# A new table of order and engines for the 3118 operations of one attention and gated-MLP kernel

## The chip, the core and the metric

The kernel runs on one core of a Trainium2 chip, in one launch. The metric is device time in microseconds; three runs of the kernel before gave 518.59, 518.84 and 520.0, with a median of 518.84. A core has five engines that work side by side, each through its own queue in order: TensorE (PE in the profile), VectorE (DVE), ScalarE (ACT), GpSimd (POOL) and SyncE (SP), which here only issues DMAs. An engine waits at an instruction until the semaphores that it names have arrived; whatever stands behind it in the same queue waits too.

## The reference, cut to what matters

Inputs are q, k, v of shape (8 batches, 8 heads, 576 positions, 64), and the weights of a gated feed-forward layer.

```python
scores = scale * np.matmul(q, k.transpose(0, 1, 3, 2))
mask_local = (rel >= 0) & (rel < stride)                                 # heads 0 to 3, stride 32
mask_strided = (rel >= 0) & (pos[None, :] % stride == pos[:, None] % stride)   # heads 4 to 7
attn = softmax(where(mask, scores, -1e9));  x = concat_heads(attn @ v)   # (8, 576, 512)
h = np.maximum(x @ w_in, 0.0);  u, v = h[..., :512], h[..., 512:]
v_n = (v - mean(v)) / np.sqrt(var(v) + 1e-06)
v_s = np.einsum('ts,bsd->btd', w_spatial, v_n) + b_spatial[None, :, None]
return (u * v_s) @ w_out                                                 # (8, 576, 512)
```

## The kernel before, in words

**What is computed where.** The heads are taken in pairs, four pairs t to a batch: pairs 0 and 1 are local, 2 and 3 strided, 32 pairs in all. For a pair TensorE makes the scores of small blocks (line 543 for local pairs, 689 for strided ones) into a PSUM bank. VectorE brings them out (580 or 705; the first four pairs with reductions at 563 and 714), ScalarE takes the exponentials (600, 726), VectorE or GpSimd divides by the sums (505), VectorE turns blocks of 32 x 32 (624, 743), and small copies, twelve for a local pair and four for a strided one (called moves here, line 405 on ScalarE and 407 on the other two), put the turned blocks into `ptl` or `pts`. TensorE then multiplies with v (653, 759), and the result is brought out as `x`.

**Two parts of a number.** The big matmuls work on rounded numbers, so each operand is kept as a rounded part and the rest. `rnd` (lines 405 and 407) writes the rounded part, with one input, on ScalarE, VectorE or GpSimd. `rest` (line 415) subtracts it from the number, with two inputs, on VectorE or GpSimd. `combine` (line 880) makes sums and differences of blocks, also with two inputs. `evac` (427 on ScalarE, 429 on VectorE) copies a PSUM bank out.

**The feed-forward part.** For each batch `v_tile` (1012) multiplies x with w_in, `chain` normalises it: relu on ScalarE (970), mean and variance on VectorE (975 to 983), a power on GpSimd (988), and the scaling on VectorE (995). `moe_1` makes u at 1212 for batches 0 to 2, `moe_u` at 1135 for batches 3 to 7. `moe_2` multiplies with w_spatial (1309, 1321, 1322), gates u with the result (1332 and 1334, VectorE), and multiplies with w_out (1413); VectorE adds the products (1441), and SyncE stores them (1434).

**What sets the order.** Every operation is recorded by `add` with the engines that may do it. Nothing plans at build time: a text `ORDER` holds one word for each of the 3118 operations. A word is the step to the next operation's number and, where there is a choice, a letter for the engine (A ScalarE, V VectorE, G GpSimd), and `*n` for n filler matmuls ahead of it. `order` reads the words and `emit` issues the operations in just that order, so the table fixes each engine's queue; it keeps every dependency in front of what needs it:

```python
n += int(step) + 1
e = dict(zip("PAVGS", ENGINES))[engine] if engine else given[0]
issued.append((n, e))
```

The buffers do not depend on the table: `Ring` hands out a fixed number of them in the order in which operations are recorded. PSUM has four banks `m`, two `s` and two `po`; SBUF has four buffers `o` and two `vv` from which results are stored. An operation that writes a ring's buffer waits for all users of what stood there before, stores included. The `port` argument of `add` names operations of VectorE and GpSimd that share a way into SBUF; nothing in this file reads it.

Of the kernel before, what the change touches and what calls it, by code (L numbers as in the profile page):

```python
# [220 lines left out]
-246G -48A 28 -106 -35 110A 302 -301A -6A -31 35A -10G 33 -34A -3V 140 144 -276A 24V -34A 270 -57 -212A 0A
127V 161 -164 -74 -51 197 -174 181A -205 121 -100G -26A 55 -54A 23G -2A -26 295 -294 23A 98 79G -151 -8A -22
28 66A -67V 66G 71V 63 -203 -31A 30 -30A 45 -162A 144 -32 19G 11 144 -203 267 -242 -161 213 -205A 201 -5 193
-197 -25 -48 71 765 -759 174 -346V 167 189 21 -235V 134 -191A 289 -235 134A -191G 201 73 -10 -14 -188 209 -79
-127 194 -78G -326 214 173 -197A 238 -430 215 -29A 241 -31 -104 -84 172 46 -246A 211 -192 177 -58V -38 140
-249A 30 170 12 -395 422 -227 230 -224 176 12A 28 -428V 245 139A 12V -71 -144 200V -178 119V 73 -78 104 -221
32 188 -104 -134 648 -413 -20 -162 -255 434 -32 -74G -119 222 -10 -138 -39 -48 210 21 -106G 628 -526 1 -451A
268 633 -679 228 -39 -72G -79 3 80V -347A 448 -28 -81V 102 -182 -12 192 -178 167 -218 123V 105 -193 -38G 189
-145 179 -197 199 -197 92A 74 -87V 115 -2 5 -197 -268V 467 -212 -256A 426 34 -238 231 -108G 2A 104 -200 -256V
462 -125A 71 -147 201 -276A 157V -344A 404 42 3 -36 -172 206 -239A 125V 115 -123V -74 81V 116 -279A -194V 415A  # L230
55 -130V 115 -43V 46 -109 116 -242A -222 284 131A 54 -249A -42 294 -61G 44 -120V 112 -207 227 -295 34A 259 -23
5 -129G -78 213 -255A 245 15 -220 -41G 243 -250A 45 85 134 -488V 469 -243A 264 -144V -2 -364 239V 267 -24
-251A 266 -138 -134A 258 17 -277V 253A -207V 23 180A -244 244V 462 -585 -122 121V 489 -485A -6 133 448 -461
411 -623 87G 133 -12 -200G 204 -120A 113 15 -136G 2A 121 4 -222A 226 -206 -16G -48A 268 -142V 3A 142 -149V
-125A 129G 483 -356 -219A 92V 2A -99G 95A 131 -223A 575 -562 217 -143G 490 -360 -143V 142 -138G 490 -334A -12
335 3 -355 -223A 226 20G 325 -479A 133 -136V -103A 243 -280 138G 140 340 -331V -255A 243 1 8G -11 12A -12 -15
22A -21 -277 47A 251G -257A 232 21V -258A 235 9 338 -331G -19 40 -20V 19 -10G -24 -227V 226 11A 20 307 -10
-319G 19 -22V -254 584 -345 -239 264V -268A 568 -308V 28 -38V 16A 22 287 -309A -7V -14G 19 -17A 16 -264 243V
-2V 22 -3A -18V 19 2A -26V 19 16 287 -320V 552 -537A 10 -8V -21A 31 -35V 18 296 -287 317 -346G 343 -322A -276
566 72 -369G -272 559 -277 320 56 -93 38 -325 -5 280 -294G 13 268 -267 319 -316 311 -329G 335 -320 311 -333V  # L240
339 -324 325 -15 -329G 297 -276 -4 308 -615A 308 274 40 -613 302 -319 15G 302 -19 309 -308 7 274G 24 -299 -298
606 32 -350 -290A -17 311 -296G -3A 886 -293 7 -300 291 -295 -8 316 -305 -306V 606 29 -350 13 -8 246 -542 565
-287 293V 0A 2G 79 -89A 0V 267 -264G -574V 565A 3G 219 -478 255A 86 -92G -568A 303 261G 32 -599 634 -310 248V
60G -635 301 302 -308 276 30 0V -30 -3A 79 -22 -300 271 21 -336 7 275V 38G 280 -284V 3G -296 254 -277 595
-244G -39V -10A -298 564 -243 -25G -4V 48 -311 265A -38 -264 296G 1V 3A -313 9 299G 43 132 -156 -322 343 -344
303 211 -31 -180 -319 527 -528 501 -15 -488 502 -486 478 -181A 12 168 -186A -314 27 468 -489 320V 156 -448
-40A 490 -141 -22 -314 484 -151V -310 -43V 38 3 271 -299 468 -443 437 -152A -314 26 287A -307 304V -3A 157
-481 19 283 -267 -38 342 -306 -38 29 7 -38V 29 292 -323V 16 495 -172G 128 -454 325A -308 447 30 37 -232V -284
476 -188 187 -474 476 5 -522 11 18 487 -519 11 509 -490 -33 315V -287 10 424 -455 20 300A -301 437 -427 471 -5
-478 430 -427 -8 2 439 -432 422 -428 437 23 -24 -444 -39 481G -433 -12 276 -270 -47A 520 -468 275A -276 426  # L250
-441 -42V 489A -5G -441 -5 6 457 -20V -439 470 -10 -503 472A -429 426V 2A -420 425V 20 -27V -432 255 190 -20A
8V -483V 534 -500 -36V 44 275 183 529 -540 -451 430A 558 -998 7 431V 71 -228A -265 -117 95 14 451 -556 113 430
-54 -373 437 -463 12 -13 6 -7 11 -6 -7A 21 -22A 0V 13 0 -6 -6 15 -16 15 -12 4 -5 10 458 -458 432 -442 31V 433
-458 -9 8 456G -461 3 21V -20 427G 25 -454 239 -4A -241 25A -19 15A -16 12A 2V -16 12G -23 9 229 -230 15G -15
# [24 lines left out]
-8 -3 12 477 -473 0 -7 -5 4 5 441V 11 -470 469 -455 441V -449 6 -13 282A -264 -8 430A 31 -2 -470 459 -453 462
# [1405 lines left out]
```

## Time and profile before

| | |
|---|---|
| median of 3 runs | 518.84 us (518.59 to 520.0) |
| profiled execution, its own time | 519.92 us |
| its span in the profile | 518.0 us |
| busy: PE, PEld, DVE, ACT, POOL | 495.0, 449.6, 414.8, 263.1, 227.1 us |
| bytes moved by DMA | 52.65 MB |
| TensorE's granted clock over the span | 0.984 of full speed |

All durations below come from that one execution. PE is the matmuls, PEld the loading of their weights beside them. A matmul's end is modelled and matmuls are pipelined, so PE counts as busy while one follows another; its idle time is what the waits list. "Idle before, releaser" says for how long an engine stood idle ahead of an instruction and what it was waiting for.

### The profile page before, as it was taken

How to read it: one execution, taken by the hardware profiler on the slowest of the kernel's cores; microseconds unless marked ns; L12 is line 12 of the kernel's file. 1: busy time of each engine (PE TensorE's matmuls, PEld its weight loads, DVE VectorE, ACT ScalarE, POOL GpSimd, SP SyncE). 2: the span in 40 equal slices, each digit the busy share in tenths (PEclk: the TensorE clock that was granted, in tenths of full speed). 3: DMA queues.
4: the chain of work that ended last, by engine and by line, in shares of the span. 5: the costliest groups of instructions: out<-in, count | busy, mean ns of one | idle time of the engine just before them, and what ended most of it. 6: DMA issues, size and time to landing. Idle time of an engine off the chain costs nothing.

```text
span 518.0 us, 14629 instructions
## 1 busy us (share of the span) xinstructions
PE 495.0 (96%) x5816; PEld 449.6 (87%) x5816; DVE 414.8 (80%) x1154; ACT 263.1 (51%) x778; POOL 227.1 (44%) x265
## 2 busy tenths in 40 slices
PE   6599999999999999988989999999999999999997
PEld 4378998889998898988889987989899998999897
DVE  5689999996676889985899779897698957895456
ACT  3699977556561686462534545354464413231221
POOL 2344566422174348462355734656146404421342
PEclk9679999999999999999999999999999999999999
DMA  8948432541304504162052503125020210011002
GB/s 274 407 177 321 153 114 77 181 137 66 101 15 126 185 2 134 27 195 71 9 171 72 185 4 122 58 84 175 1 97 1 79 56 2 0 35 59 0 1 92
DMA packets 26244, 52.65 MB, mean 102 GB/s; under 512 B 3136, under 2 KB 11584, under 8 KB 26176
## 3 DMA queue, kind: packets, MB, share of 16 engines
q1 hardware_dynamic: 26176, 51.72, 30.0%
q8 instruction: 46, 0.75, 0.6%
q14 instruction: 22, 0.18, 0.1%
HBM read 42.27 MB, written 9.44 MB: 100 GB/s over the span
## 4 chain that ended last, share of the span: by engine, by line
PE 67%; DVE 17%; issue 4%; DMA 4%; POOL 3%; ACT 3%; SPq 2%; DVEq 0%; POOLq 0%; ACTq 0%
PE m L1413 15%; PE m L1012 14%; PE m L1309 11%; PE m L1135 10%; PE m L1212 5%; PE po L653 3%; PE s L543 3%; PE po L759 2%; DVE vv L995 2%; SPq L435 2%; POOL bn L988 2%; DVE bn L975 1%; DVE vn L415 1%; DVE ptl L407 1%; PE m L1321 1%
## 5 line engine op out<-in xcount | busy, mean ns | idle before, releaser
L1309 PE MATMUL m<-wsp_sb,vn 128*128 128x288 f32 x720 | 108.8, 297 | 2.3 <-DVE u L1334 2.2
L1012 PE MATMUL m<-w_in_sb,x 128*128 128x512 f32 (+1 forms) x408 | 106.0, 403 | 2.7 <-ACT x L427 2.1
L1309 PEld LDWEIGHTS m<-wsp_sb,vn 128*128 128x128 f32 x720 | 100.0, 189 | 5.1 <-DVE u L1334 3.0
L1012 PEld LDWEIGHTS m<-w_in_sb,x 128*128 128x128 f32 (+1 forms) x408 | 74.1, 188 | 19.8 <-ACT x L427 2.2
L988 POOL TENSOR_TENSOR bn<-bn,sel 128x1 f32<-128x1 f32 (+1 forms) x37 | 24.8, 674 | 93.7 <-DVE bn L983 93.7
L600 ACT ACTIVATE pl<-pl,ml 128x64 f32<-128x64 f32 (+1 forms) x140 | 47.7, 341 | 30.7 <-DVE ml L580 30.3
L1413 PE MATMUL m<-g,w_out_sb 128*128 128x288 f32 x384 | 60.2, 298 | 2.0 <-DVE o L1441 1.6
L1413 PEld LDWEIGHTS m<-g,w_out_sb 128*128 128x128 f32 x384 | 53.6, 188 | 3.9 <-DVE o L1441 2.3
L405 ACT COPY ptl<-pc 32x320 f32<-32x320 f32 (+3 forms) x112 | 40.3, 361 | 16.1 <-DVE pc L624 14.3
L970 ACT ACTIVATE vv<-m 128x512 f32<-128x512 f32 (+1 forms) x37 | 22.0, 596 | 43.1 <-PE m L1012 27.4
L1413 PE MATMUL m<-vn,w_out_sb 128*128 128x288 f32 x288 | 42.8, 299 | 0.8 <-DVE vn L415 0.4
L1212 PE MATMUL m<-x,w_in_sb 128*128 128x288 f32 x288 | 41.6, 298 | 0.0
L1413 PEld LDWEIGHTS m<-vn,w_out_sb 128*128 128x128 f32 x288 | 39.3, 188 | 2.4 <-DVE vn L415 0.7
L1212 PEld LDWEIGHTS m<-x,w_in_sb 128*128 128x128 f32 x288 | 39.8, 188 | 1.5
L975 DVE BATCH_NORM_STATS2 bn<-vv 128x6 f32<-128x512 f32 (+1 forms) x37 | 25.4, 685 | 15.7 <-ACT vv L970 15.3
L415 POOL TENSOR_TENSOR g<-u,g 128x576 fp32r<-128x576 f32 (+1 forms) x24 | 29.3, 1224 | 17.4 <-ACT g L405 14.9
L995 DVE TENSOR_SCALAR vv<-vv,bn 128x512 f32<-128x512 f32 (+1 forms) x37 | 25.2, 683 | 8.2 <-POOL bn L988 7.9
L405 ACT CAST g<-u 128x576 fp32r<-128x576 f32 (+1 forms) x30 | 16.9, 584 | 24.7 <-DVE u L1334 19.1
L580 DVE CUSTOM_DVE_ANT_0 pl<-s,cst_sb 128x64 f32<-128x64 f32 (+1 forms) x140 | 26.0, 206 | 1.3 <-PE s L543 1.2
L600 ACT ACTIVATION_READ_ACCUMULATOR pl<-pl,ml 128x1 f32 (+1 forms) x140 | 26.3, 188 | 0.0
L1146 DVE TENSOR_TENSOR u<-m,vv 128x288 f32<-128x288 f32 x30 | 13.6, 455 | 13.4 <-PE m L1135 12.3
L1334 DVE SCALAR_TENSOR_TENSOR u<-u,m 128x288 f32<-128x288 f32 x36 | 15.1, 445 | 10.1 <-PE m L1322 10.0
(230 smaller groups left out, 1061.1 us busy)
## 6 DMA issues: line engine op xcount, KB each, us to landing
q<-qT SPq DMA_DIRECT2D x30, 295.0 KB, 3.6
outT<-o SPq DMA_DIRECT2D x48, 144.0 KB, 2.4
k<-kT SPq DMA_DIRECT2D x16, 304.0 KB, 4.2
kbd<-ks SPq DMA_DIRECT2D x32, 144.0 KB, 4.1
v_raw<-vl SPq DMA_DIRECT2D x11, 384.0 KB, 4.1
v_raw<-vs SPq DMA_DIRECT2D x8, 512.0 KB, 4.3
xt<-vs SPq DMA_DIRECT2D x7, 512.0 KB, 4.8
outT<-vv SPq DMA_DIRECT2D x16, 144.0 KB, 1.9
```

Of the source, the lines that this page charges most:

```text
L405: eng.copy(dst(), src())
L415: eng.tensor_tensor(dst(), src(), f32(hi()), op=ALU.subtract)
L580: eng.tensor_tensor_reduce(out=p_sb()[:m, u, :], in0=s_ps[u % 2]()[:m, f0 : f0 + 2 * STRIDE], in1=msk[:m], scale=-SCALE, scalar=3.0e38, op ...
L600: eng.activation(p_sb()[:m, u, :], src, AF.Exp, bias=st()[:m, u : u + 1], scale=SCALE if masked else -1.0, **total,)
L975: lambda eng: eng.bn_stats(bn()[:m, 0:6], v()[:m]), [(v,)], [(bn,)],
L988: lambda eng: eng.tensor_tensor(bn()[:m, 9:10], bn()[:m, 8:9], sel[:m, 0:1], op=ALU.pow),
L995: lambda eng: eng.tensor_scalar(v()[:m], v()[:m], bn()[:m, 6:7], bn()[:m, 9:10], op0=ALU.subtract, op1=ALU.mult),
L1012: eng.matmul(v_ps()[:m, :], x_at(kt)[:, a, :], w_in_sb[:, w, kt, HF:], start=(n == 0 and i == 0), stop=(n == NT - 1 and i == 2),)
L1135: eng.matmul(o_ps()[:, :HS], w_at(w)[:, a * P : (a + 1) * P], x_at(j), start=first and kk == 0 and i == 0, stop=kk == 1 and i == 2, skip_g ...
L1212: eng.matmul(u_ps()[:, :HS], w_in_sb[:, w, kt, f * P : (f + 1) * P], xs[NHP * b + kt]()[:, a, r], start=(n == 0 and i == 0), stop=(n == NT ...
L1309: eng.matmul(s_ps()[:, :HS], vn()[:, a, kt, fs], wsp_sb[:, w, kt, r], start=(kt == 0 and i == 0), stop=False,)
L1413: eng.matmul(o_ps()[:, :HS], w_out_sb()[:, b_at, w, kk, a * P : (a + 1) * P], at(j, kk), start=first and kk == 0 and i == 0, stop=kk == 1 ...
```

## The change

Only the text `ORDER` is replaced, all of its lines. The operations, their tiles, their dependencies and the buffers stay. The first line of each:

```diff
@@ -213,123 +213,123 @@
 ORDER = """
-182 -178G 3V -6 8 -6V 23 -32 4G 5A -13 10V 21 0 -28V 54 -2 121 0V -81 80 -81 -96V 24 -33 -2 185 -3V -151*6 118
+32 -28G -2 2V 53 -51V -12 7G -8 60 -54G 23 -24G 23 -23G 169 5 -186 2G -5 102 -41*4 -2 89 -47 -2 -4 -69 0 138
...
```

Read with the recorded operations, the new table gives 425 of them another engine. From and to: VectorE to GpSimd 99, GpSimd to VectorE 82, ScalarE to GpSimd 80, VectorE to ScalarE 66, ScalarE to VectorE 63, GpSimd to ScalarE 35. VectorE has 993 operations after 1013, ScalarE 594 after 636, GpSimd 321 after 259. By kind:

| kind | VectorE | ScalarE | GpSimd |
|---|---|---|---|
| two inputs (`rest`, `combine`) | +9 | 0 | -9 |
| rounding (`rnd`, whole tiles) | -6 | -23 | +29 |
| moves into `ptl` and `pts` | -18 | -11 | +29 |
| bringing out (`evac`) | +7 | -7 | 0 |
| division by the sums (505) | -5 | 0 | +5 |
| all others | -7 | -1 | +8 |

TensorE has the same 1014 operations and SyncE the same 196 DMAs, both in another order; the fillers are 4 and 3 where they were 6 and 1.

**The first loads, on SyncE.** `w_out_sb<-qT`, `kbd` and, later, `xt` belong to the strided pair that is done first; the first `k` and `q` to the first local pair (pair 1), the second `q` and `k` to pair 0; `vn` and `u` are staging room for w_in. Before:

```order
L435 DMA vn_81<-w_in 128x1024
L435 DMA w_out_sb_89<-qT 128x590
L435 DMA o_91<-eye 128x128
L435 DMA cst_sb<-cst 128x192
L435 DMA kbd<-ks 64x576 x2
L435 DMA k_0_101<-kT 128x608
L435 DMA q_0_103<-qT 128x590
L435 DMA q_0_107<-qT 128x590
L435 DMA k_0_110<-kT 128x608
L435 DMA xt_113<-vs 128x1024
```

Now, after a first row `w_out_sb_81<-qT`:

```order
L435 DMA q_0_86<-qT 128x590
L435 DMA cst_sb<-cst 128x192
L435 DMA o_91<-eye 128x128
L435 DMA k_0_93<-kT 128x608
L435 DMA kbd<-ks 64x576 x2
L435 DMA vn_101<-w_in 128x1024
L435 DMA u_103<-w_in 128x1024
L435 DMA k_0_111<-kT 128x608
L435 DMA kbd<-ks 64x576
L435 DMA q_0_131<-qT 128x590
L435 DMA vn_101<-w_in 128x1024
L435 DMA xt_167<-vs 128x1024
```

The w_in load has gone from first place to behind the first local pair, and pair 0's q and k, and `xt`, now stand behind two and three w_in loads.

**VectorE ahead of the first gate of batch 3.** `u` is the gate (1334), `vv` and `vn` the end of the normalising of the same batch, `ptl`, `pp` and `mx` attention for later batches, `x_10` blocks for a later batch. Before:

```order
L995 TENSOR_SCALAR vv_3995<-vv_3995,bn_4004 128x512
L880 TENSOR_TENSOR x_10_3173<-x_10_3173 128x2x288
L415 TENSOR_TENSOR vn_3876<-vv_3953,vn_3876 128x512
L415 TENSOR_TENSOR vn_3876<-vv_3995,vn_3876 128x512
L705 SCALAR_TENSOR_TENSOR pp_69<-s_3961,cst_sb 128x16x18
L407 TENSOR_SCALAR ptl<-pc_3955 32x8x32
L705 SCALAR_TENSOR_TENSOR pp_70<-s_4052,cst_sb 128x16x18
L407 TENSOR_SCALAR ptl<-pc_3955 32x10x32
L714 TENSOR_REDUCE mx_4121<-pp_69 128x16
L714 TENSOR_REDUCE mx_4127<-pp_70 128x16
L1334 SCALAR_TENSOR_TENSOR u_3750<-u_3750,m_3907 128x288
```

Now:

```order
L415 TENSOR_TENSOR vn_3888<-vv_3922,vn_3888 128x512
L995 TENSOR_SCALAR vv_3939<-vv_3939,bn_3949 128x512
L720 TENSOR_TENSOR pp_69<-pp_69,mx_4032 128x16x18
L407 TENSOR_SCALAR ptl<-pc_3975 32x4x32
L407 TENSOR_SCALAR ptl<-pc_3975 32x2x32
L415 TENSOR_TENSOR vn_3888<-vv_3939,vn_3888 128x512
L407 TENSOR_SCALAR ptl<-pc_3975 32x10x32
L407 TENSOR_SCALAR ptl<-pc_3975 32x4x32
L880 TENSOR_TENSOR x_10_3248<-x_10_3248 128x2x288
L880 TENSOR_TENSOR x_10_3248<-x_9_2831,x_10_3248 128x2x288
L1334 SCALAR_TENSOR_TENSOR u_3740<-u_3740,m_3932 128x288
```

Between the last `vn` and the gate stood six operations, and now four stand there.

**SyncE at the stores of batch 2's results.** `outT<-` are stores from `o` and `vv`; `v_raw`, `xt`, `q` and `k` are loads for later pairs. Before:

```order
L1434 DMA outT<-vv_3421 128x288
L435 DMA v_raw_9_3670<-vl 128x768
L1434 DMA outT<-o_3556 128x288
L1434 DMA outT<-o_3583 128x288
L435 DMA kbd<-ks 64x576
L1434 DMA outT<-vv_3433 128x288
L435 DMA xt_3708<-vs 128x1024
```

Now:

```order
L435 DMA q_14_3498<-qT 128x590
L1434 DMA outT<-o_3509 128x288
L1434 DMA outT<-vv_3395 128x288
L1434 DMA outT<-vv_3477 128x288
L1434 DMA outT<-o_3568 128x288
L435 DMA v_raw_9_3731<-vl 128x768
L435 DMA xt_3736<-vs 128x1024
```

Both `vv` stores now stand ahead of the load of `v_raw`.

## Rows read from the trace of the kernel before

**Rows 1.** Part 1 of the page: busy us, share of the span, instructions.

```profile
PE 495.0 (96%) x5816; PEld 449.6 (87%) x5816; DVE 414.8 (80%) x1154; ACT 263.1 (51%) x778; POOL 227.1 (44%) x265
```

**Rows 2.** Stretches: length, busy by engine, TensorE's granted clock, DMA share, GB/s.

```profile
0.00:13.00 13.00, 8.56 (x221) 5.47 (x222) 7.67 (x21) 4.18 (x7) 3.53 (x9) 0.92 0.82 274
13.00:26.00 13.00, 6.83 (x131) 4.22 (x114) 8.21 (x21) 8.38 (x31) 5.10 (x11) 0.63 1.04 408
24.00:32.00 8.00, 7.35 (x38) 5.45 (x38) 8.00 (x19) 7.72 (x22) 3.17 (x5) 0.57 0.81 305
26.00:100.00 74.00, 73.36 (x1091) 65.48 (x1092) 70.85 (x229) 62.45 (x197) 41.17 (x53) 0.96 0.49 168
200.00:300.00 100.00, 95.00 (x1211) 89.00 (x1210) 84.38 (x239) 45.63 (x140) 50.63 (x53) 1.00 0.33 103
```

**Rows 3.** Waits of PE from 0 to 30 us: total, times, longest.

```profile
PE s L543 <- issue: 3.4, 1, 3.4
PE m L1012 <- ACT x L427: 2.1, 1, 2.1
PE m L543 <- DMA q<-qT: 2.0, 1, 2.0
```

**Rows 4.** Waits of PE from 30 us to the end, the longest and the last of ten.

```profile
PE m L1309 <- DVE u L1334: 2.2, 3, 1.5
PE m L1413 <- DVE o L1441: 1.9, 3, 1.1
PE m L1135 <- DVE vv L429: 1.4, 1, 1.4
...
PE m L1135 <- DVE o L1441: 0.2, 1, 0.2
```

**Rows 5.** Groups by form: count, then busy us, mean ns, idle us before.

```profile
L415 DVE TENSOR_TENSOR vn<-vv,vn 128x512 fp32r<-128x512 f32 x23 | 16.0, 704 | 0.7 <-POOL vn L407 0.5
L415 DVE TENSOR_TENSOR vn<-u,vn 128x576 fp32r<-128x576 f32 x11 | 10.6, 982 | 0.1
L415 DVE TENSOR_TENSOR g<-u,g 128x576 fp32r<-128x576 f32 x11 | 10.2, 928 | 0.3 <-POOL g L407 0.2
L407 DVE TENSOR_SCALAR ptl<-pc 32x64 f32<-32x64 f32 x20 | 6.6, 328 | 0.5
L407 DVE TENSOR_SCALAR pts<-pc 32x288 f32<-32x288 f32 x15 | 6.3, 423 | 0.4
L429 DVE COPY x<-po 128x288 f32<-128x288 f32 x14 | 6.2, 444 | 0.0
L505 DVE TENSOR_TENSOR pp<-pp,mx 128x288 f32<-128x288 f32 x9 | 5.6, 621 | 0.0
L880 DVE TENSOR_TENSOR x<-x 128x576 f32<-128x576 f32 x6 | 4.5, 756 | 0.0
L415 POOL TENSOR_TENSOR g<-u,g 128x576 fp32r<-128x576 f32 x13 | 20.3, 1568 | 16.6 <-ACT g L405 14.5 <-DVE g L407 2.2
```

**Rows 6.** Time line, 232 to 237 us: start, us, engine, operation, idle before.

```profile
232.04 0.33 SPq L1434 DMA_DIRECT2D outT<-vv  x1
232.62 1.43 POOL L415 TENSOR_TENSOR g<-x,g 128x576 fp32r<-128x576 f32 x1 [1.36 <-ACT g L405]
232.81 1.92 DVE L505 TENSOR_TENSOR pl<-pl,ml 128x640 f32<-128x640 f32 x1
234.01 1.98 POOL L415 TENSOR_TENSOR vn<-x,vn 128x576 fp32r<-128x576 f32 x1
236.04 0.46 DVE L429 COPY vv<-m 128x288 f32<-128x288 f32 x1 [1.30 <-DMA outT<-vv]
```

**Rows 7.** Time line of DVE, 263 to 267 us, ahead of the gate.

```profile
263.35 1.46 DVE L407 TENSOR_SCALAR ptl<-pc 32x256 f32<-32x256 f32 x1
...
265.22 1.53 DVE L407 TENSOR_SCALAR ptl<-pc 32x320 f32<-32x320 f32 x1
```

**Rows 8.** Time line of PE, 10 to 24 us.

```profile
12.08 1.17 PE L543 MATMUL s<-k,q 64*32 64x64 f32 x64 [0.28 <-DMA k<-kT]
16.70 0.44 PE L543 MATMUL s<-k,q 64*32 64x64 f32 x8 [3.44 <-issue]
18.59 2.19 PE L759 MATMUL po<-pts,xt 128*64 128x72 f32 x32
23.75 0.73 PE L1012 MATMUL m<-w_in_sb,x 128*128 128x512 f32 x2 [2.08 <-ACT x L427]
```

More of the change, by code (lines that the diff above doesn't have):

```diff
@@ L221 @@
[L221 to L230, printed above, removed]
@@ new lines @@
+62 -57 -4 -71*3 67 -34 94G -59 -9 2 -27V 2A 63 -62G -45A -3V 44G -4A -40 31G 1A 70 36 -16G -92A -39 142 -36
+-72A 312 -59 -221 36 -105G 48 -15A 321 -253 54 -131A -74 110 37 -38 -32A 122 -92V 136 -167 57 -101 208G -102
+173 -211 -28 -3A 65G -142 173 -141 73A 14 -17A 7G -38V 323 -287G -7A -35 37G -36 25A 308 -304G -6V 5A 0G 277
+-283A 132 -208A 81 204G -181 178 -79G -124 -132 185 -31A 177 55 -259A 122G -127V 25A 51 -21 -31A -28 23A -22
+54G 225 -78 -3A -122 -3 43 -210V 110 30 23 122G -119 -3 2 0 -31 235 -201 -66A 18V 34 187 -245A 167G -166 163
@@ new lines @@
+-17G 18 335 3 -343 -265 276 -11A 5V 4 -31G 2A 346 -331 -268 278 323 -330A -27G 390 -653 570 51 -360V 389 -360
+-38G 32 -291A 813 -523 317 -346V 300 -266 -21G 342 -332 2 317 -313 -21V 4V 9 -15G 343 -333 332 -331 4 312
+-332G 13 278 -275 267 -265 -4 268 -266 310 -608 292 5 -316A 16G 295 315 -311 -10 304 -598 304 353 -358 -317
+559 -546A 1G 305 -327 312 -295A 1G 293 304 -36 -266 2 262 -266 335 -71V 43 -610 301 490 -228 -287 377 -92V 4A
+3G -574V 574A -2G -8A -277 10 269G 34 -38A 0G -574V 567A -264 329 -69A 2V -256 -315 1 312 341 -23 -310 331
@@ new lines @@
+-23G -321 342V -355 303G 50 -344 -12 330 -311 -21 10 475 -476 0 256 -270 329 196 -515 481 -224 29 225 -252
+-248 474 -203A 27 -331 592 -94 -15 -486 350 -312 270A 279 -321A -260 5 -18 266A 53 178 -230 -271G 38 460 -520
+29 15 540 -267G 192 73 -527 261V 0G -290 -17V 299G -274 456 7 -476 470 -140 -339V 27 266A 20 -316V 286A -257 0
+258A 24G -63 -220 438 -137 -42G -270 261V -275 278G -290 22 447 35 -33 -475 309 153 17 -172G -21 -282 508
+-208G -19 -284 14 -26 509 -189 -312 504 -489 491 -4 -227V 254 -515 261A -258 274A -18 -267 -18 454 38 -215
@@ new lines @@
+608 -425 409A -438 27 4 418V -452A 0G 19 -5 410A -427V 30 -188A 156G 30 395A -296V -108 404A -416 420G -8A
+-411 -179V 593G -420 432 -430 -12G 16 407A 15 -19A -432G 30 361V 31A -394 -32V 18 406A 37 -625G 179 -178A 605
+-418 -25G 16 439 125 -559 -8 565 -554 410 -417 -191V 552 53G -417 666 -667 -195G -274 470 -449 444 -32G 50A
+-17 638 -636 13A 382 -401 15V -8 0 7G 405 -421 -9 8 0 418V -425 87G 320 -404 25 -32 31 -27 2 7V 15A -24 413
+-414 12G 12 -26 21 -17G 19 -4 -10V 523 -126 -399A -7V 369 34 -77A 208 32 -571G 13V -18A 373 159 -515A 517
@@ new lines @@
+23 -593 -8 166 -167 6 591 0 -593 626 -468A -160 157V 404A -585 21 625 236 -863 594 -618 11A 650 -73V -566 -4
+158A -170G 599 34 -622 -27 588A 30 -594 155A 399V -402A -4G 422 -580V 4 156A -6G -157V 12 -9 156G -3G -147 -9
+172A -165 608V -444A -175 589 -590 589 -583 -8 589V -437 -147 164G -19 397A -545 164A -19 -147 0 -11 176 412
+-590G 154 -146 -10V 180 448 -463V -14 -146 546 310 -574G -140 -146A 547 -403 473 -456 413A 17 -451 -147V 174
+425 -51 -376 -30 12V 385A -795 417 -10A 420G -406 442 213 -687 437A -406 563 -162A -420 118V 302A 158 -576
@@ new lines @@
+-224 11V -24 5 443V -444 16V 426 -444 -8 23G 384A -409 413A -405 -10 9 -5 6 9V -13 2 -3 2 8V -9 415 -416 17G
+-6A 6 -20 19 -14G 14 -14V 11A 1 -16G 422 -35 -374A 407 -415V -9A 14 -12V 11 -16G 421 -405 -3A 2 2V -19A 12 8
+-25V 17A 6 -23G 401A -387 7 -2 358A 0 -365A 5 -8G 390 -383 -2 2 354V -355 387V -383 362G -369 2 -15V 7 372G
+-361 -10 9 155G -164 7 -7 6 0 157A -166 160G 7 -169 6 353G -352 151V -149 -7 2 151V -155 354 -353 148V -149
+157 208 -209 -4 -5V 14 -11A -5V -152 366A -209 209V -2A -217G -152 158 205A -201 -165 158A 6 -190 178A 10 -3
@@ L333 @@
+-10 -17G 60 -52 20 -15 31 -39V 25 -20 -7G 30 -12 -14 0 23 -24 4 0 -6 15 -16A 9 16 -27V 42 -29 5 0 4 -24 0 4 -5
+21 -6 5 -19 19 -20 3 32A -33 20 -21 13 -9 8 16V 0A -18 0 -6 21G -14 -4 7 -5 4 7V -13 4 -5 24 -8V -14 6G 13 -21
+21 -2A -13V 13 -17A 5V 11 -2A 1 -17A 6V 11 -22V 18A 2 -20V 16 8 -24V 16A 6 -7 -15V 21 -26G 23 3 -11A 7 -26V 27
+-10G 6 7 -6 -12V 11 -11G 15 -6 3 -4 4 3 -9 4 3 -4 5 0 -7 8 -3 5 -11 4 5 -5 -7 10 -5 4 -5
 """
```

188 lines of the change are left out of this document (82 added, 106 removed).

## The prediction

> **What bounds the kernel now.** I read part 1 of the page first: matmuls keep PE busy for 495.0 of 518.0 us, DVE is busy for 414.8, ACT for 263.1 and POOL for 227.1 [rows 1]. The change leaves PE its 1014 operations, so it can win only what PE waits, and the next views are PE's waits and the stretches.
>
> From 0 to 26 us PE is busy for 8.56 + 6.83 = 15.4 us and stands still for 10.6 us, while the DMA engines are full: share 0.82, then 1.04, at 274 and 408 GB/s [rows 2]. Three waits make 7.5 of that: 3.4 us in the scores of the second local pair, put down to "issue" (nothing that the profile shows), 2.1 us for ACT's copy of x in front of the first v tile, and 2.0 us for a load of q [rows 3]. From 24 to 32 us PE hardly rests, but its granted clock is 0.57 of full speed, a mix of the two levels, 1.2 and 2.4 GHz; it costs (1 - 0.57) x 8 = 3.4 us [rows 2].
>
> From 30 us on ten kinds of wait are listed. They begin with 2.2, 1.9 and 1.4 us, each behind DVE, end with 0.2, and sum to 8.7 us, of which 7.5 are for DVE [rows 4]. So after the start the kernel runs at PE's pace with 8.7 us lost to VectorE's being late here and there. That, and the start, is the room.
>
> Why is DVE late? One place shows it. At 232.62 a subtraction on POOL starts and takes 1.43 us, to 234.05. At 232.81 DVE starts a division of 128x640 that takes 1.92 us, and the nearest two-input row, of 576 elements, takes 0.756. POOL's next subtraction, started at 234.01, lasts to 235.99 where the first took 1.43 [rows 6]. Each stood still while the other worked. The same shape shows it in the mean: 0.756 us at line 880, but 0.928 and 0.982 in 11 + 11 subtractions of line 415 [rows 5], which is 11 x 0.172 + 11 x 0.226 = 4.4 us lost in these 22 instructions alone. And two moves of 32x256 and 32x320 elements take 1.46 and 1.53 us [rows 7] where 32x288 takes 0.423 in the mean [rows 5].
>
> **The change part by part. The work moved.** DVE gives up 18 moves, mostly 13 of 32x64 and 7 of 32x288 (13 x 0.328 + 7 x 0.423 = 7.2 us, with 0.5 gained in other sizes), and 5 divisions (5 x 0.621 = 3.1). It gives up roundings, shifts and clearings for 2.8 + 2.6 + 1.8 = 7.2 us, by the means of their own forms. It takes on 7 copies out of PSUM (7 x 0.444 = 3.1), and two-input operations: four more of 512 (4 x 0.704 = 2.8), three of 576 (3 x 0.756 = 2.3), and smaller ones for 1.7 [rows 5]; two subtractions of maxima add 1.3. The sum is -6.7 - 3.1 - 7.2 + 3.1 + 6.8 + 1.3 = -5.8 us of DVE's time. ACT loses 42 operations, some 19 us; it is idle half of the time and PE waits for it 1.2 us after the start, so I count nothing. POOL gains 62 operations and by the same means 27 us, to 254 of 518. All of this lies beside PE's matmuls, and what it is worth shows only in PE's waits.
>
> The Trainium skill, "SBUF — State Buffer", section "SBUF: two separate sides", says that VectorE and GpSimd share one pair of ports as a lock held for the whole instruction, while ScalarE's port is its own. The 1.92 us and 1.98 us agree [rows 6]. It speaks against part of this change: 79 roundings and moves go from ACT to POOL, from a port of their own to the shared one. By it DVE would lose more than before; what that makes is the second rival.
>
> **The start.** The load of q for the first local pair stands behind 512 + 295 + 64 + 96 + 288 + 304 KB; with its own 295 that is 1854 KB. Now it and its k are in front, and the scores wait only for the strided pair's `kbd`, at 1342 KB. 512 KB at 274 GB/s are 1.9 us, so the 2.0 us wait goes [rows 2, 3]. The second pair's q, k move from 2453 to 3109 KB: 656 KB, 2.4 us later at 274 GB/s and 1.6 at 408. Its scores began at 12.08 and, with the 3.44 us, ended at 17.14 [rows 8]; now they begin at 13.7 to 14.5 and end at 15 (no such wait) or 19.5 (the same one). The first pair's softmax no longer stands behind the second's reductions on DVE, but its division does. `xt` moves from 2965 to 4133 KB, which at 408 GB/s is 2.9 us; its matmuls began at 18.59, some time after the load, and I count nothing. So the first v tile, at 23.75, comes between 3.9 us sooner (both waits short) and 2.4 later. I take -1.5 us: the q wait gone, part of it given back by the second pair.
>
> **The steady part.** Two of the waits can be followed. The gate at 266 us, 1.5 us [rows 4], stood behind the two long moves, 263.35 to 266.75 [rows 7]; now two moves and two differences stand there, 0.328 + 0.423 + 2 x 0.756 = 2.3 us if POOL does not block them, against 3.4 for the moves alone. I count the 1.5 as gone. The 1.4 us at 236 [rows 4]: PE waited for DVE's copy into `vv`, and that for a store issued at 232.04, with loads round it [rows 6]. The `vv` stores now precede `v_raw`, and this copy is ACT's. I count it as gone. The other waits, 8.7 - 2.9 = 5.8 us, move with the order and can't be followed one by one. DVE has 5.8 us less to do, but a new order makes waits of its own; I let 1.6 of the 5.8 go. Together -4.5 us; the bounds are -8.7 (all gone) and +4.5 (what the third rival costs).
>
> **The end and the queues.** The last products are the same, in another order: the last two sums on DVE and two stores. I count nothing, and up to half a microsecond (one sum of 0.45) either way. SP's queue moves are in the terms above; a store behind two loads costs some microseconds only if a buffer waits for it.
>
> **The sum.** The profiled execution took 519.92 us: 518.0 of span and 1.9 round it. 519.92 - 1.5 - 4.5 = 513.9. It lay 1.08 above the median of 518.84; carried over to the median, 512.8 us.
>
> **The rivals. First, more goes than I allow**: if the collisions fall and all 8.7 us of waiting go, and the start gains 3.0, the time is 518.84 - 11.7 = 507.1. For it: DVE is the releaser of 7.5 of the 8.7. Against it: DVE is still busy for some 409 us in a stream that PE paces, and from 26 to 100 us it is busy for 70.85 of 74 [rows 2], so a little lateness remains.
>
> **Second, the lock takes back what the moves give.** POOL holds the ports 27 us longer, 12% more. In the 22 instructions above DVE lost 4.4 us; if all that is blocked is ten times as much (an estimate: VectorE has some 400 operations that are recorded with `port`), 12% of 44 is 5.3 us, all but the 5.8 saved. Then the steady waits only change place, and with the start at -1.5 the time is 517.3; with the start at 0, 518.8. This is the page's rule at work. Against it: most of what POOL takes is short and with one input, and it gives up 9 two-input holds of about 1.5 us [rows 5].
>
> **Third, slower: PE waits for POOL.** POOL has 54 of the `ptl` moves where it had 29. Each of the local pairs' products at 653 needs all twelve moves, and one move that lands behind a subtraction of 1.43 to 1.57 us [rows 5, 6], itself blocked at times, holds PE if it comes after PE's other work is through. If that strikes 7 of the 14 later local pairs with 1.5 us each, 10.5 us come on top of -6.0: 523.3. It decides from the point where a POOL move is the last of the twelve; the order alone puts three or four per pair there. For it: a POOL hold grows to 1.98 us when DVE blocks it [rows 6]. Against it: POOL is the releaser of none of PE's waits [rows 3, 4].
>
> That the change does not do what it says can be left out: the table fixes every queue.
>
> **How the numbers follow.** Forecast 0.50, its own range 508.5 to 516.5; more gained 0.15; lock takes it back 0.17, centred on 517.8; PE waits for POOL 0.18. A measurement here can tell about 0.3%, 1.6 us, from no change: faster is below 517.3, slower above 520.4. Faster: 0.15, nearly all of 0.50, and a little of the second, 0.66. Same: most of the second and a little of the others, 0.15. Slower: 0.19. The range reaches from 506 to 521; it takes in the first rival's time, all of the second and the near edge of the third. The clock adds to its width: a stretch at the lower level as in 24 to 32 us, gone or twice as long, is 3.4 us either way.
>
> **What would show it.** Right: PE's first scores at 543 with no wait for q; the first v tile some 1 to 2 us before 23.75; no wait of PE for DVE's 1334 above 1 us near 264 us; the waits after 30 us at about 4 us; DVE's 576-element subtractions nearer to 0.756 than 0.928 and 0.982. Wrong: the "issue" wait grown or moved behind the later load; POOL `ptl` moves as the releaser of 653; busy DVE above 414.8 in spite of less work; more waits for stores.

## The result, and the profile after

The changed kernel takes 505.04 us (median of four runs, 504.79 to 506.25) against 519.42 for the kernel before in the same session (518.59 to 521.45). The ratio is 0.972, with an interval of 0.969 to 0.976: 14.4 us less, where 6.0 were forecast. The profiled execution took 504.79 us, 503.0 of them span.

First part 1 of the page of the changed kernel (against [rows 1]), then its stretches, with the columns of [rows 2].

```profile
PE 490.7 (98%) x5816; PEld 449.0 (89%) x5816; DVE 398.7 (79%) x1133; ACT 245.3 (49%) x736; POOL 254.8 (51%) x328
```

```profile
0.00:13.00 13.00, 8.68 (x154) 5.59 (x155) 4.85 (x14) 4.27 (x12) 5.03 (x13) 1.00 0.84 298
13.00:26.00 13.00, 11.44 (x271) 7.89 (x272) 12.27 (x28) 11.83 (x35) 9.95 (x16) 0.74 0.77 285
24.00:32.00 8.00, 7.62 (x195) 5.64 (x190) 7.88 (x22) 7.56 (x17) 7.32 (x11) 1.00 1.00 380
200.00:300.00 100.00, 99.17 (x1250) 92.53 (x1250) 81.79 (x247) 46.32 (x149) 49.78 (x59) 1.00 0.34 106
```

From 13 to 26 us PE is busy for 11.44 us where it was 6.83; POOL has gone from 5.10 to 9.95 there. From 200 to 300 us PE rests 0.8 us instead of 5.0. DVE's busy time has fallen by 16.1 us, where the forecast counted 5.8.

PE's waits, first from 0 to 30 us (the longest; against [rows 3]), then all from 30 us to the end (against [rows 4]):

```profile
PE s L543 <- DMA q<-qT: 2.4, 1, 2.4
PE m L517 <- ACT o L1515: 1.0, 1, 1.0
PE m L1600 <- DVE zeros L1553: 0.9, 1, 0.9
PE s L543 <- issue: 0.8, 1, 0.8
```

```profile
PE m L1413 <- DVE o L1441: 1.1, 3, 0.4
PE m L1135 <- DVE ml L580: 0.8, 1, 0.8
```

Ten kinds of wait with 8.7 us have become two with 1.9. In the start the "issue" wait is 0.8 instead of 3.4, ACT's copy of x is gone from the list, and the wait for q now stands at the second pair. PE's time line (start, us, line, idle before) answers to [rows 8]:

```profile
13.01 1.05 PE L543 MATMUL s<-k,q 64*32 64x64 f32 x67 [2.38 <-DMA q<-qT]
14.82 0.43 PE L543 MATMUL s<-k,q 64*32 64x64 f32 x5 [0.77 <-issue]
17.88 2.19 PE L759 MATMUL po<-pts,xt 128*64 128x72 f32 x32
20.83 0.72 PE L1012 MATMUL m<-w_in_sb,x 128*128 128x512 f32 x2
```

The first v tile begins at 20.83 us, 2.9 earlier. Part of that, and of the 2.0 us wait for q, belongs to the one execution of the kernel before: in two runs below that keep its first loads (new rest; halves in the old table) the wait is 0.7 and 0.4 us and the tile comes at 23.0 and 22.8.

**Where DVE's 16 us come from.** Groups by form, of forms with as many instructions in both kernels (count, busy us, mean ns, idle before), in the kernel before and then in the changed one:

```profile
L995 DVE TENSOR_SCALAR vv<-vv,bn 128x512 f32<-128x512 f32 x35 | 23.9, 686 | 7.5 <-POOL bn L988 7.2
L505 DVE TENSOR_TENSOR pl<-pl,ml 128x640 f32<-128x640 f32 x9 | 8.5, 943 | 0.2
L496 DVE TENSOR_SCALAR mx<-mx 128x16 f32<-128x16 f32 x16 | 5.8, 368 | 0.1
L407 DVE TENSOR_SCALAR ptl<-pc 32x256 f32<-32x256 f32 x8 | 4.6, 575 | 0.2
```

```profile
L995 DVE TENSOR_SCALAR vv<-vv,bn 128x512 f32<-128x512 f32 x35 | 20.8, 593 | 7.7 <-POOL bn L988 7.4
L505 DVE TENSOR_TENSOR pl<-pl,ml 128x640 f32<-128x640 f32 x9 | 7.6, 845 | 0.2
L496 DVE TENSOR_SCALAR mx<-mx 128x16 f32<-128x16 f32 x16 | 3.5, 220 | 0.0
L407 DVE TENSOR_SCALAR ptl<-pc 32x256 f32<-32x256 f32 x8 | 2.3, 290 | 0.2
```

These 68 instructions alone take 3.1 + 0.9 + 2.3 + 2.3 = 8.6 us less, with shape and count unchanged. They are among those that fell most: over all 906 instructions of such forms the fall is 10.1 us, and some forms rose. An operation of 16 elements that falls from 368 to 220 ns did not get less work; that it stands still less often is so far a reading (the halves below take it to 307 ns in the old order). But the large subtractions, at which the prediction looked, did not gain as a class (against [rows 5]; the last row's shape was at 756 ns):

```profile
L415 DVE TENSOR_TENSOR vn<-u,vn 128x576 fp32r<-128x576 f32 x11 | 9.6, 875 | 0.2 <-POOL vn L407 0.2
L415 DVE TENSOR_TENSOR g<-u,g 128x576 fp32r<-128x576 f32 x12 | 11.8, 992 | 0.7 <-ACT g L405 0.7
L880 DVE TENSOR_TENSOR x<-x 128x576 f32<-128x576 f32 x7 | 6.7, 962 | 0.0
```

### The profile page after: what moved, and what is told of

Read it like the earlier page. It is cut to its first block, busy times and chain, and to the rows that moved or that the text cites. A ratio compares the mean times of both kernels' runs of the same rounds, so it can differ in the third digit from the quotient of the medians.

```text
span 503.0 us, 14630 instructions
## 1 busy us (share of the span) xinstructions
PE 490.7 (98%) x5816; PEld 449.0 (89%) x5816; DVE 398.7 (79%) x1133; ACT 245.3 (49%) x736; POOL 254.8 (51%) x328
## 4 chain that ended last, share of the span: by engine, by line
PE 88%; DVE 4%; ACT 2%; POOL 2%; DMA 1%; issue 1%; SPq 1%; DVEq 0%; POOLq 0%; ACTq 0%
PE m L1309 19%; PE m L1012 19%; PE m L1413 16%; PE m L1135 11%; PE m L1212 7%; PE po L759 3%; PE po L653 3%; PE s L543 2%; PE s L689 2%; PE m L1321 2%; PE m L1322 2%; DMA q<-qT 1%; DVE o L1441 1%; PE s L1309 1%; PE po L1309 1%
## 5 line engine op out<-in xcount | busy, mean ns | idle before, releaser
L1309 PE MATMUL m<-wsp_sb,vn 128*128 128x288 f32 x720 | 106.2, 297 | 0.0
L1012 PE MATMUL m<-w_in_sb,x 128*128 128x512 f32 (+1 forms) x408 | 103.8, 398 | 0.3 <-DVE x L415 0.3
L1012 PEld LDWEIGHTS m<-w_in_sb,x 128*128 128x128 f32 (+1 forms) x408 | 72.7, 185 | 16.6 <-DVE x L415 0.7
L405 ACT COPY ptl<-pc 32x320 f32<-32x320 f32 (+3 forms) x98 | 35.5, 363 | 15.0 <-DVE pc L624 8.8
L415 POOL TENSOR_TENSOR g<-u,g 128x576 fp32r<-128x576 f32 (+1 forms) x21 | 26.3, 1258 | 23.3 <-ACT g L405 15.4
L407 POOL TENSOR_SCALAR ptl<-pc 32x64 f32<-32x64 f32 (+3 forms) x58 | 23.6, 407 | 10.5 <-DVE pc L624 6.1
L995 DVE TENSOR_SCALAR vv<-vv,bn 128x512 f32<-128x512 f32 (+1 forms) x37 | 21.8, 590 | 7.7 <-POOL bn L988 7.4
L1334 DVE SCALAR_TENSOR_TENSOR u<-u,m 128x288 f32<-128x288 f32 x36 | 15.6, 449 | 12.8 <-PE m L1322 12.6
L405 ACT CAST g<-u 128x576 fp32r<-128x576 f32 (+1 forms) x24 | 13.8, 582 | 17.8 <-DVE u L1334 13.9
```

Of the source, the lines that this page charges most:

```text
L405: eng.copy(dst(), src())
L407: eng.tensor_scalar(dst(), src(), 1.0, 0.0, op0=ALU.mult, op1=ALU.add)
L415: eng.tensor_tensor(dst(), src(), f32(hi()), op=ALU.subtract)
L1012: eng.matmul(v_ps()[:m, :], x_at(kt)[:, a, :], w_in_sb[:, w, kt, HF:], start=(n == 0 and i == 0), stop=(n == NT - 1 and i == 2),)
L1309: eng.matmul(s_ps()[:, :HS], vn()[:, a, kt, fs], wsp_sb[:, w, kt, r], start=(kt == 0 and i == 0), stop=False,)
```

## Experiments

Every time stands beside a ratio to runs of the kernel before on the same chip, with its 95% interval. "New" and "old" are the tables after and before.

### Where in the run: start or rest

```diff
-ORDER: 3118 words of one table
+ORDER: the first 200 operations of the new table, then the others as in the old one   (e1)
+ORDER: the first 200 operations of the old table, then the others as in the new one   (e2)
```

> The new table's first 200 operations (the engines work on them until about 32 us), then all others in the old order on the old engines. Theory A (two separate gains: about 5 of the 15 us of span come from the first 32 us, its clock included, about 10 from the steady part): 514.4 us, first v tile at 1012 near 20.8 us, waits of PE after 30 us still near 8.7 us, busy DVE near 414. Theory B (the start's lead is eaten up by the first waits behind it, because the old order's DVE is late there anyway): 517 to 519. Theory C (most of the gain is the stretch at the lower clock that is gone): 509 to 511 with a clock of 0.99.

> The old table's first 200 operations (about 35 us), then all others in the new order on the new engines. Theory A: 509.5 us, with the first v tile near 23.75 us, the clock at 24 to 32 us near 0.57 as before, PE's waits after 35 us at about 2 us, and busy DVE at 399 to 402. Theory B: 505 to 507 (the start adds nothing). Theory C: 514 to 516.

Measured: new start 517.86 us, ratio 0.998 (0.997 to 1.000); new rest 510.72, ratio 0.985 (0.983 to 0.987). So the rest alone is worth 8 us, the start alone 1, and together 14.4. The same start that gives 1 us in front of the old rest gives some 6 in front of the new one (510.72 against 505.04; by the spans 508.3 against 503.0, 5.3). In the first run a part of the lead was lost at the seam, in a wait that neither table has (a longest wait of PE after 30 us; this text of the table is four lines shorter, so line 1008 is 1012 elsewhere):

```profile
PE m L1008 <- POOL w_in_sb L411: 1.9, 1, 1.9
```

Theory A holds for the rest; for the start it holds only in front of the new rest, and in front of the old one theory B does (517 to 519). Theory C, the clock, falls: in the first run the granted clock was 1.00 over the whole start, where the changed kernel has 0.50 from 14 to 20 us, and both reach the first v tile at 20.8 us.

### Engines without order, order without engines

```diff
-word: step and engine from one table
+old steps, new letters: 425 words like 3V -> 3G, -3V -> -3A   (e3)
+new steps, old letters                                        (e4)
```

> The old order of all operations with the new table's engines. Theory L (the gain behind the start is that DVE and POOL are blocked by each other for less time, which needs order and engines together): busy DVE stays at 410 or more (5.8 us less work, collisions as before or more, since POOL does 27 us more), time 515 to 519. Theory W (DVE has less to do, whatever the order): busy DVE 405 to 409, time 510 to 514.

> The new order of all operations with the old table's engines. Theory L: collisions as many as in the kernel before or more, busy DVE 412 to 420, time 511 to 516 (the start's 5 us gained, the rest not). Theory W: the same DVE work as before in an order that suits it, busy DVE 414, time 514. Theory O (the order of DVE and SP alone removes the waits, engines do not matter): 505 to 508, with waits of PE after 30 us near 2 us.

Measured: engines alone 541.14 us (1.043, 1.041 to 1.046), order alone 534.77 (1.031, 1.029 to 1.033). Both are far slower than either whole table, which no theory had. DVE's busy time, in the page of each:

```profile
PE 503.3 (94%) x5816; PEld 450.6 (84%) x5816; DVE 417.5 (78%) x1133; ACT 245.9 (46%) x736; POOL 261.0 (49%) x328
```

```profile
PE 500.2 (94%) x5816; PEld 452.0 (85%) x5816; DVE 422.1 (79%) x1154; ACT 262.1 (49%) x778; POOL 227.6 (43%) x265
```

The first has exactly the changed kernel's instructions on each engine, and DVE needs 417.5 us for them where it needs 398.7 in the new order. So how long DVE takes for its work is a property of order and engines together, as theory L has it. But L's times (515 to 519, 511 to 516) are missed by some 20 us, and DVE's 2.7 and 7.3 us above the 414.8 of before can't make 22 and 16 us. PE's listed waits after 30 us are 21.5 and 19.0 us instead of 8.7, behind several engines; with the new engines in the old order 3.4 us of them are for POOL's moves in front of 653. The rest is not placed.

### Is it the blocking? Holds halved at the same order

```diff
-eng.tensor_tensor(dst, a, b)                     # on GpSimd
+for i in range(2): eng.tensor_tensor(half(dst, i), half(a, i), half(b, i))   # 256 elements a partition or more
```

> The kernel before, with each of GpSimd's subtractions, sums and divisions of 256 elements a partition or more issued as two instructions of half the size (a hold of 1.4 us becomes two of 0.75; GpSimd works longer by some 0.1 us each). Theory L (in the old order the 10 us of the steady part are lost because DVE stands still for a whole GpSimd operation): DVE's blocked time falls by a third or more, DVE's busy time from 414.8 to 400 to 408, time 511 to 516. Theory D (which operation stands behind which decides, not how long DVE is held): within 2 us of the kernel before, 517 to 521.

> The same halving in the changed kernel. Theory L: DVE's busy time falls from 398.7 to below 392 and the time to 503 to 504.5. Theory D: 504.5 to 507, a little slower if anything by GpSimd's extra instructions.

Measured: in the old table 513.66 us, ratio 0.989 (0.986 to 0.993), 5.7 us faster; in the new table 506.13, about 1 us slower than the changed kernel. The page of the first, and all its waits of PE after 30 us:

```profile
PE 494.8 (97%) x5816; PEld 450.4 (88%) x5816; DVE 403.1 (79%) x1154; ACT 263.4 (51%) x778; POOL 257.9 (50%) x401
```

```profile
PE m L1413 <- DVE o L1441: 1.8, 1, 1.8
PE po L653 <- ACT tail L405: 1.8, 2, 1.3
PE m L1413 <- POOL vn L407: 0.4, 1, 0.4
PE m L1135 <- DVE vv L429: 0.4, 1, 0.4
PE m L1321 <- DVE tail L415: 0.3, 1, 0.3
PE m L1135 <- ACT vv L427: 0.2, 1, 0.2
```

Order and engines are those of the kernel before, POOL even works 31 us longer, and yet DVE is busy for 11.7 us less, PE's listed waits fall from 8.7 to 4.9 us, and the time falls. Length of hold is what changed. So in the old table shorter holds alone are worth 5.7 us (theory L holds). In the new table the same halving takes only 2.3 us off DVE's busy time (396.4) and gains nothing (theory D holds). That the 5.7 us are part of the 8 that the new rest gains is argued from these two runs and not shown. What is left, 2 us or so, I put down to the order; no run shows it alone.

### Is it DVE's busy time as such?

```diff
+if n in EXTRA: self.extra(n)      # behind 60 of POOL's, or 50 of DVE's, own operations; the first clears junk
+gpsimd.tensor_tensor(junk[:, 0:184], junk[:, 0:184], junk[:, 0:184], op=add)      # d1, new table
+gpsimd.tensor_tensor(junk[:, 9:10], junk[:, 8:9], junk[:, 6:7], op=pow)           # d2, new table
+vector.bn_stats(junk[:, 178:184], junk[:, 0:178])            # d4, new table; bd4, old table
```

> The changed kernel with 59 added POOL additions of 128x184 elements (two inputs, on a scratch tile that nothing else reads; one clearing of it first), one behind every fourth or fifth of POOL's own operations between about 45 and 460 us; some 59 x 0.55 = 32 us of POOL. Theory L (DVE stands still while POOL holds the shared way into SBUF, and that lateness reaches PE): DVE's busy time grows by 5 to 12 us though its instructions are the same, and the time is 3 to 8 us above that of the run with 59 powers: 508 to 514 us. Theory W (only the work in each queue counts; blocking is a small matter): DVE's busy time grows by under 3 us and the time equals that of the run with 59 powers within 1.5 us.

> The control: the same places in POOL's queue, but each added operation is a power of 128x1 (0.67 us in the kernel's own rows, 59 x 0.67 = 40 us of POOL), which moves almost no data. Both theories: DVE's busy time within 1 us of 398.7, time 505 to 507; what it is above 505.0 is the cost of delaying POOL's own operations.

> The changed kernel with 50 added statistics of 128x178 elements on DVE (one input, of the kind that line 975 has and whose time does not spread in the trace), spread from about 45 to 460 us: some 50 x 0.25 to 0.3 = 12 to 15 us of DVE, about as much as DVE's blocked time fell from before to after (414.8 - 398.7 = 16 us). Theory L (a us of DVE's time is worth most of a us of the program, so that the 16 us explain the steady part's 10): 512 to 517 us. Theory O (order: with this order DVE has slack, and the gain is not its busy time but which operation comes last): 505 to 508 us.

> The kernel before with 50 added statistics of 128x178 on DVE, placed as in the changed kernel, where they made DVE 11 us busier and cost 1.2 us. Theory O (in the old order the operations for which PE waits stand behind others in DVE's queue, so what is added in front of them reaches PE; in the new order they stand early): 523 to 530 us. Theory D (DVE's time matters little in either order; the old waits are places where one operation stands behind the wrong one): 519 to 521.5, as cheap as in the new order.

Measured: POOL additions 509.09 us (0.979, 0.977 to 0.981); powers 506.56 (0.975, 0.972 to 0.977); statistics in the new table 506.22 (0.974, 0.972 to 0.976); in the old one 520.46 (1.002, 1.000 to 1.004). The pages of the first and third:

```profile
PE 491.5 (97%) x5816; PEld 448.1 (88%) x5816; DVE 408.7 (81%) x1133; ACT 244.9 (48%) x736; POOL 289.9 (57%) x388
```

```profile
PE 490.0 (97%) x5816; PEld 448.2 (89%) x5816; DVE 409.8 (81%) x1182; ACT 245.0 (49%) x736; POOL 254.8 (51%) x329
```

Ten more us on DVE by blocking cost 4 us, of which 2.5 are beyond the control; the control, in which POOL works as long (292.0 us), makes DVE 3.6 us busier itself, so the 2.5 stand against 6.4 us of DVE. Eleven by work of its own cost 1.2, and ten in the old table as little. So theory L as I had put it (a us of DVE's time is most of a us of the program) falls, in both tables, and so does theory O for the old one (523 to 530). I read this as: what counts is where DVE stands still, in front of an operation for which PE waits, not its sum. No run moves one such stop from one place to another.

### The start: ScalarE and the loads

```diff
-94G -62G 44G 31G ...     +94A -62A 44A 31A ...     new table: all 80 back on ScalarE (p1), 14 early ones (p2)
-6A -64A -235A 110A ...   +6G -64G -235G 110G ...   old table: the same 14 on GpSimd (b1)
```

> The changed kernel, with the 80 operations that went from ScalarE to GpSimd (roundings and moves with one input) put back on ScalarE at the same places of the order. The second rival of the prediction (these 80 block DVE and take back part of the gain): DVE's busy time falls by 3 to 6 us and the time to 501 to 504 us. Theory N (they cost nothing where they stand): 504 to 506. Theory A (ScalarE was late with them, so that the move itself is part of the gain): 507 to 512, with PE waits for ACT in the list.

> The changed kernel with only the 14 of those 80 operations back on ScalarE that run before about 50 us (nine moves into ptl at 18 to 27 us, one later, and four roundings of weights and vn). Theory S (ScalarE is full from 20 to 32 us in the kernel before, 5.80 and 5.84 us of 6, and these moves are what the first local products wait for; in the run with all 80 back PE's matmuls were 3.5 us late by 60 us): 508 to 510 us, PE busy for under 9 us of 20 to 32 where the changed kernel has 10.8. Theory R (the later 66 are what cost 6 us, by making ScalarE's queue late in the steady part): 505 to 506.5.

> The mirror of it: the kernel before, old order and old engines, with only the same 14 operations on GpSimd. Theory S: 515.5 to 517.5 (2 to 3.5 us gained in the start), PE busy for more of 20 to 32 us. Theory T (the old order of loads holds the start up, not ScalarE): 518 to 520. Third: slower, 521 to 525, since the old order has GpSimd do them late and every edit of engines in that order made new waits.

Measured: 511.01 us (0.983, 0.981 to 0.985) with all 80 back, 508.57 (0.979, 0.977 to 0.981) with the 14 back, 523.81 (1.009, 1.007 to 1.011) in the old table. So on ScalarE 14 of the 80 cost 3.5 us and the other 66 cost 2.4. The page with all 80 back:

```profile
PE 491.0 (96%) x5816; PEld 448.2 (88%) x5816; DVE 398.4 (78%) x1133; ACT 277.8 (55%) x816; POOL 210.9 (41%) x248
```

POOL works 44 us less than in the changed kernel, and DVE's busy time is the same (398.4 against 398.7 us): where they stand in the new order, these 80 operations cost DVE nothing. The stretch from 20 to 32 us, in the kernel before, the changed one, and with the 14 back:

```profile
20.00:32.00 12.00, 9.27 (x116) 7.12 (x113) 10.96 (x23) 11.65 (x36) 5.05 (x9) 0.67 0.88 337
```

```profile
20.00:32.00 12.00, 10.83 (x272) 7.88 (x270) 11.61 (x32) 11.28 (x26) 11.01 (x17) 0.99 0.81 291
```

```profile
20.00:32.00 12.00, 7.62 (x189) 5.63 (x181) 9.06 (x24) 11.53 (x33) 5.27 (x7) 1.00 0.85 299
```

ScalarE, "idle half of the time" over the span, is full here: 11.65 of 12 us, while POOL works 5.05. The new table takes POOL to 11.01. With the 14 back PE is busy for 7.62 us and waits for just these moves:

```profile
PE po L653 <- ACT ptl L405: 2.8, 2, 1.6
```

In the old order the same 14 operations make it slower, by 4.5 us. In the first 60 us PE's listed waits sum to 10.7 us, as before: a POOL move (1.2) and ACT's relu (1.3) are new, the wait for q is 0.2. After 60 us they sum to 11.0 instead of 8.7; the rest of the 4.5 is not placed.

```diff
-SyncE's DMAs in one table's order
+all 196 in the old order, new table for the four other engines   (asp)
+the first 18 in the old order, new table                          (as1)
+the first 18 in the new order, old table                          (bs1)
```

> The changed kernel with SyncE's 196 DMAs in the old order; the queues of the four other engines are untouched. The prediction's terms for the loads (2.0 us for q in the start, 1.4 us for the store of vv at 236 us): 507 to 509 us, with a wait for q in front of the first local scores and the strided first scores later. Theory E (loads are hidden, engines and order of the others make the gain): 505 to 506. Theory F (the order of loads is most of the start's 5.3 us): 510 to 512.

> The changed kernel with only SyncE's first 18 loads in the old order (w_in first, pair 0's q and k ahead of two w_in loads), the rest and the four other engines as they are. Theory F (in the start the new order of loads is worth most of 5.3 us, since with all the old loads the first v tile came at 23.6 us and PE was 3.7 us late at 60 us): 508 to 510.5 us, first v tile near 23.6 us. Theory S (ScalarE's relief is the start, loads little): 505.5 to 507.

> The mirror: the kernel before with only the first 18 loads in the new order. The prediction's term for the start (-1.5 us: the 2.0 us wait for q gone, part given back by the second pair): 516.5 to 518. Theory J (a part of the new table alone gains nothing, since the other queues wait in the old order): 518.5 to 522.

Measured: 529.00 us (1.018, 1.015 to 1.020), 508.29 (0.978, 0.974 to 0.983) and 522.69 (1.006, 1.004 to 1.008). The first 18 loads are worth 3.3 us in the new table, and their cost shows at the same two waits as before the change:

```profile
16.94 0.43 PE L543 MATMUL s<-k,q 64*32 64x64 f32 x5 [3.44 <-issue]
20.00 1.61 PE L759 MATMUL po<-pts,xt 128*64 128x72 f32 x32
24.86 3.30 PE L1012 MATMUL m<-w_in_sb,x 128*128 128x512 f32 x6 [2.55 <-ACT x L427]
```

In the old table the new loads cost 3.9 us: PE waits 5.4 us for ACT's negated copy of `eye` (line 1515), which stands in ACT's queue behind an operation that itself waits 6.5 us for the load of w_in, now later.

```profile
PE m L517 <- ACT o L1515: 5.4, 1, 5.4
PE m L1012 <- ACT x L427: 3.7, 1, 3.7
```

With all loads old, another 20 us go, more than any theory had, 12.6 of them in listed waits between 60 and 200 us. There, as I read it, loads stand in SyncE's queue behind stores that are not due yet: two stores of `o` held the queue for 38.2 us, in the changed kernel for 22.4. PE's longest waits from 60 to 200 us, then SyncE's row:

```profile
PE m L1212 <- ACT vv L970: 5.4, 2, 3.5
PE s L543 <- DMA k<-kT: 3.8, 1, 3.8
PE s L543 <- DMA q<-qT: 2.7, 2, 2.0
```

```profile
SPq L1434 <- ACT o L427: 38.2, 2, 20.3
```

### The clock, and a try at more

```diff
-306        +306*7         old table: seven fillers ahead of the first v tile   (bf)
-71*3       +71*1          new table: one filler ahead of line 759, and          (i1)
+L500, L743 ahead of L861, L850 on DVE; the four moves into pts ahead of a rounding on ACT and a subtraction on POOL
```

> The kernel before with seven more filler matmuls in front of the first v tile, in PE's idle time from 21.4 to 23.5 us; nothing else. Theory K (the second stretch at the lower clock, 24.35 to 31.18 us, costs 3.4 us and comes from PE's idling in front of it): granted clock in 24 to 32 us above 0.9 instead of 0.57, time 515 to 516.5. Theory M (PE in that stretch waits for ScalarE and VectorE, both busy for 5.8 to 6 us of 6 there, and a faster clock only makes it wait more): clock higher but time within 1 us of before.

> The changed kernel with the first strided pair's reciprocal and transpose ahead of the two shifts of w_in on DVE, its four moves ahead of a rounding on ScalarE and a subtraction on GpSimd, and one filler instead of three in front of line 759. If the first strided pair sets the start: line 759 begins at 16 to 16.8 us instead of 17.64 and the time falls to 503.5 to 504.5. If w_in's parts or the load of v do: 505 to 506.

Measured: 519.48 us, ratio 1.000 (0.998 to 1.001), and 506.65, ratio 0.976 (0.973 to 0.978). With the fillers:

```profile
24.00:32.00 8.00, 7.11 (x58) 5.15 (x59) 8.00 (x20) 7.72 (x22) 2.78 (x3) 1.00 0.73 276
```

The clock is 1.00 instead of 0.57 and PE is busy for 7.11 us instead of 7.35 [rows 2]: DVE works 8.00 of the 8 us and ACT 7.72, so PE finishes a tile sooner and waits for the next. Theory M holds; the stretch at the lower level cost nothing that these runs can tell (0.2% is 1 us). In the last run line 759 began at 16.42 us instead of 17.88, as meant, but the first v tile at 21.58 instead of 20.83, after 1.88 us of waiting for DVE's copy of x: the shifts that had been put back stood in front of it. The chain was not what set the start. No version here beat the changed kernel.

## Why the prediction was wrong

The direction was right; the time lies just below the range, and the gain is 2.4 times the forecast. Both large terms were too small.

**The start, -1.5 us: measured 5 to 6** in front of the new rest. The q wait went and the "issue" wait nearly so, as the first case had it. The step that failed is "ACT loses 42 operations, some 19 us; it is idle half of the time ... so I count nothing". The half is a mean over the span. From 20 to 32 us ScalarE was full, and PE's largest wait there was for it [rows 3]; 14 moves and roundings less on it are worth 3.5 us. Also "`xt` ... I count nothing" and the term for the loads failed: the loads were read as two single waits, while the 18 loads are worth 3.3 us, through the strided pair's end and the first v tile. The two do not add up (3.5 + 3.3 is more than 5.3): undoing either one loses more than half of the start's gain. The term that the forecast did count, 2.0 us for q, was read from one execution; with the same loads it was 0.4 and 0.7 in two others.

**The steady part, -4.5 us: measured 8** (10 by the profiles' spans, which put the start at 5). The two waits that I followed went, for the reason given: no wait for 1334 is listed any more, nor one for `vv`. The four operations ahead of the gate take 2.0 us, from 252.08 to 254.12, where 2.3 were forecast, and ACT's copy into `vv` waits for PE and no longer for a store. The step that failed is "The other waits ... can't be followed one by one ... I let 1.6 of the 5.8 go": of the 5.8, 3.9 went. The bound was tight as well. PE's list held 8.7 us, hardly more than was gained, but the same waits stand longer in the list of its weight loads, which come first; there, from 36 us on, those not put down to "issue" sum to 15.7 us before and 2.3 after, a fall of 13.4 that overstates the gain as the first list understates it. The first rows of before, and the first such row of after:

```profile
PEld m L1309 <- DVE u L1334: 3.0, 3, 1.7
PEld m L1413 <- DVE o L1441: 2.8, 4, 1.3
...
PEld m L1135 <- DVE vv L429: 1.6, 1, 1.6
```

```profile
PEld m L1413 <- DVE o L1441: 1.3, 2, 0.7
```

**The work moved, -5.8 us of DVE: measured -16.1.** The sum was made at the means of before, so it took the collisions as given; they fell by some 10 us. I had seen 4.4 us of collisions in 22 instructions and scaled them up in the second rival, with the wrong sign. The first rival comes nearest: collisions fell, 6.8 of the 8.7 us of waits went and the start gained more than its 3.0; its 507.1 is 2.1 us above the result. The second rival, that POOL's 27 us more would block DVE more, falls: it scaled blocking with POOL's hours. With the same engines and the old order it would have been right on DVE's busy time (417.5 us); with the new order it was not, and there the 80 operations that came from ACT, 44 us of POOL, cost DVE 0.3 us. The rule behind it, that the lock is held for the whole instruction (the Trainium skill, "SBUF — State Buffer", section "SBUF: two separate sides"), the runs bear out for the two-input operations: halving them freed 11.7 us of DVE in the old table. What it costs is another matter, which order and engines decide.

**The third rival** falls: POOL releases none of PE's waits after 30 us, though moves go to it. Its mechanism is real in the old order, where the new engines make PE wait 3.4 us for POOL's moves. **The clock**, 3.4 us either way in the range, was worth nothing that the runs can tell. **The end** and the queues gave no more than was said.

## What to carry to other kernels

Read an engine's load in the stretch that sets the time: an engine at 51% of the span can be full for the 12 us that hold the start back. Between two engines that block each other, ask not only for work and hours but for which operations meet; splitting the long holds at unchanged order is a cheap test of what blocking costs. And parts of a table that was laid out as a whole can't be priced one at a time in the old one: the new rest alone gained 8 us, but engines alone, order alone, first loads alone and early moves alone made it slower, by 22, 16, 4 and 4.5 us.

## What was not expected of the hardware

Powers of one element a partition on POOL, meant as a control that leaves the shared way alone, still made DVE 3.6 us busier over 59 of them (402.3 against 398.7); whether by blocking or by shifting POOL's other operations is open. TensorE's clock differs between executions with the same first 200 operations: 0.50 from 14 to 20 us in one, 1.00 in the other, with no difference in when the first v tile began.
